# Token halves on TensorE's row tiles, a later second layer, and softmax rows with heads in pairs, in a dynamic convolution with a feed-forward network

## The chip, the cores and the metric

The kernel runs on one core of a Trainium2 chip. The metric is the device time of one execution in microseconds; 881.08 us is the median of three executions before the change (879.11 to 881.46). The profile is of one further execution, whose own time is 880.54 us.

## The reference

A softmax over seven taps per token and head gives the weights of a causal convolution over the last seven tokens; each head weights its own 24 of the 192 channels. The result goes through a feed-forward layer with a squared ReLU.

```python
w = exp(weight_gen - max); w = w / sum(w)                 # (8, 4096, 8 heads, 7 taps)
out[b, s, h, :] = sum_k w[b, s, h, k] * x_pad[b, s + k, h, :]   # 8 heads x 24 channels
h = maximum(out.reshape(32768, 192) @ w_in, 0)            # w_in 192 x 2048
y = (h * h) @ w_out                                       # w_out 2048 x 192, result f32
```

## The kernel before

The 32768 tokens are cut into 64 blocks of 512 (`j`), eight to each of the eight batch entries (`jb` is the place of a block in its entry).

**Softmax.** Per batch entry one table `vd` in DRAM holds, for each token, eight slots per head, of which seven are the normalised weights, skewed so that a row can be read as a band. `exp` runs on ScalarE (L139), the sum and the reciprocal on VectorE (L146, L152), and `scale` (L160) multiplies on GpSimd and writes the result skewed into `v_big`: neighbouring taps land 64 fp16 apart, each value alone. `store` (L172) sends it to DRAM over the queue of SyncE (SP). The first entry is done in four parts of 1024 tokens (`parts`), the first two parts of which stand ahead of the loop and the last two at the start of blocks 0 and 1. Every later entry is done in five chunks during blocks 0 to 4 of the entry before it.

**Convolution.** A block reads its band rows `wr` (SP queue) and its tokens `xt` (GpSimd's queue) three blocks ahead. VectorE multiplies `wr` with a 0/1 mask into a banded matrix `bd` (L223), and TensorE multiplies it with `xt` (L251): 80 small matmuls in four column tiles of 32 columns. Channels 0 to 127 stand in bank 0 of `yp`; channels 128 to 191 stand in bank 1 twice, on partitions 0 to 63 and again on 64 to 127. ScalarE copies both banks to fp16 `y` (L264).

**Feed-forward.** `h` is made in eight pairs of 128 columns (`fp` 0 to 7), each two PSUM banks. The lower matmuls (L274) contract channels 0 to 127 over 512 tokens; the upper ones (L282) contract channels 128 to 191, with the two column groups of a pair side by side in the two 64-row halves of the array. ReLU is on ScalarE (L293), the square on VectorE (L299), the second layer on TensorE (L310), and the result leaves PSUM through VectorE (L320).

**Order.** Every engine runs its instructions in the order in which the code issues them. The eight pairs go in three groups, 0 to 2, 3 to 5, 6 and 7; the second layer of a group is issued behind the first layer of the next group. PSUM has three buffers of two banks, which `h` and `yp` share in turn (`ps_h`), and one for the output `o` (`ps_o`). In the third group the convolution of the next block stands behind both layers' matmuls of that group. In this text lower, upper, conv and second layer are the lines L274, L282, L251 and L310.

## Time and profile before

| | |
|---|---|
| median of three executions | 881.08 us |
| the profiled execution, its own time | 880.54 us |
| its span, first to last instruction | 878.8 us |
| TensorE matmul busy | 796.8 us (91%) |
| VectorE busy | 638.2 us (73%) |
| ScalarE busy | 568.2 us (65%) |
| GpSimd busy | 147.6 us (17%) |
| mean granted TensorE clock | 0.991 of 2.4 GHz |

The span is the time between the first and the last instruction of the core; the execution's own time also has what lies around it. Busy time is the union of the instructions' times, and an instruction's time has its latency in it, so two neighbours on one engine overlap by about 0.1 us (VectorE, ScalarE) or more (TensorE). Idle time is put down to the instruction that ended it.

### The profile page before, as it was taken

The numbers are of one execution on the slowest core, as the hardware profiler recorded it, in microseconds if no ns is written. First come the engines' busy times: TensorE is split into PE (matmuls) and PEld (weight loads), VectorE is DVE, ScalarE is ACT, GpSimd is POOL, SyncE is SP. The second block draws the span as 40 slices with busy tenths as digits, with TensorE's granted clock in tenths as the row PEclk, the third lists the DMA queues.
The fourth block names the chain that finished last, engine by engine and source line by source line (L and its number), as shares of the span: only waits on it lengthen the run. The fifth ranks groups of instructions, "written<-read, shape, count | busy, mean of one in ns | idle before, by whom it ended". The sixth has DMA issues, their size and how long they took to land.

```text
span 878.8 us, 25261 instructions
## 1 busy us (share of the span) xinstructions
PE 796.8 (91%) x11264; PEld 520.6 (59%) x11264; DVE 638.2 (73%) x979; ACT 568.2 (65%) x616; POOL 147.6 (17%) x140
## 2 busy tenths in 40 slices
PE   0678999989998999998999899998999899999997
PEld 0345666655665666665665665665666566666665
DVE  2567787687768787678777778668776878767674
ACT  0346666666676666666666666666667666666764
POOL 5332120123002220112201212012300212000000
PEclk9889999999999999999999999999999999999999
DMA  9522372232713254033622237223271225433111
GB/s 165 116 47 39 60 156 54 37 68 57 141 46 50 52 116 103 25 67 53 144 56 57 35 63 156 48 44 67 51 148 46 45 57 92 78 47 68 41 38 37
DMA packets 123789, 63.03 MB, mean 72 GB/s; under 512 B 87713, under 2 KB 121120, under 8 KB 122912
## 3 DMA queue, kind: packets, MB, share of 16 engines
q0 software_dynamic: 44480, 17.57, 18.0%
q1 hardware_dynamic: 79200, 43.84, 17.4%
q8 instruction: 88, 1.44, 0.7%
q14 instruction: 21, 0.17, 0.1%
HBM read 49.60 MB, written 29.36 MB: 90 GB/s over the span
## 4 chain that ended last, share of the span: by engine, by line
PE 45%; DVE 24%; ACT 14%; issue 13%; DMA 2%; POOL 1%; ACTq 0%; SPq 0%; DVEq 0%; POOLq 0%
PE o L310 23%; PE h L274 12%; DVE g L299 9%; ACT t L293 8%; DVE bd L223 7%; PE h L282 7%; ACT y L264 4%; DVE o_sb L320 4%; PE yp L251 3%; DVE ssum L146 3%; DVE rcp L152 2%; ACT wg L139 2%; DMA wr<-vd 1%; POOL mask L92 0%; DMA vd<-v_small 0%
## 5 line engine op out<-in xcount | busy, mean ns | idle before, releaser
L293 ACT ACTIVATE t<-h 128x1024 f16<-128x1024 f32 x512 | 489.8, 1023 | 282.3 <-PE h L282 264.9
L299 DVE TENSOR_TENSOR g<-t 128x1024 f16<-128x1024 f16 x512 | 383.1, 775 | 102.1 <-ACT t L293 102.1
L310 PE MATMUL o<-w_o,g 128*128 128x192 f16 x4096 | 380.5, 248 | 47.8 <-DVE g L299 41.6
L310 PEld LDWEIGHTS <-g 128*128 128x128 f16 x4096 | 331.8, 98 | 116.4 <-DVE g L299 81.0
L274 PE MATMUL h<-y,w_a 128*128 128x512 f16 x1024 | 259.7, 382 | 8.1 <-ACT t L293 6.9
L223 DVE TENSOR_TENSOR bd<-wr,mask 128x832 f16<-128x832 f16 (+2 forms) x320 | 171.0, 582 | 17.9 <-DMA wr<-vd 17.9
L160 POOL TENSOR_TENSOR v_big<-wg,rcp 128x448 f16<-128x448 f32 (+1 forms) x35 | 81.6, 2330 | 474.2 <-DVE rcp L152 474.2
L274 PEld LDWEIGHTS <-w_a 128*128 128x128 f16 x1024 | 97.9, 98 | 91.0 <-issue 20.0
L282 PE MATMUL h<-y,w_b 64*128 64x512 f16 x1024 | 144.5, 381 | 0.0
L146 DVE TENSOR_REDUCE ssum<-wg 128x64 f32<-128x448 f32 (+2 forms) x39 | 24.7, 633 | 110.0 <-ACT wg L139 110.0
L282 PEld LDWEIGHTS <-w_b 64*128 64x128 f16 x1024 | 34.3, 94 | 97.2 <-issue 82.2
L251 PE MATMUL yp<-bd,xt 128*32 128x104 f16 (+7 forms) x5120 | 71.1, 210 | 21.6 <-DVE bd L223 21.6
L251 PEld LDWEIGHTS <-xt 128*32 128x32 f16 (+3 forms) x5120 | 59.5, 93 | 48.8 <-issue 35.5
L213 POOL DMA_DIRECT2D xt<-in_x_dram x56 | 49.7, 887 | 170.8 <-PE yp L251 170.8
L264 ACT CAST y<-yp 128x1024 f16<-128x1024 f32 x64 | 65.1, 1018 | 19.3 <-PE yp L251 19.3
L320 DVE COPY o_sb<-o 128x768 f32<-128x768 f32 x64 | 60.8, 950 | 3.9 <-PE o L310 1.0
L139 ACT ACTIVATE wg<-wg 128x448 f32<-128x448 f32 (+2 forms) x39 | 23.6, 610 | 2.0 <-DMA wg<-in_weight_gen_dram 2.0
L152 DVE RECIPROCAL rcp<-ssum 128x64 f32<-128x64 f32 (+2 forms) x39 | 22.1, 566 | 1.7
L160 POOL TENSOR_TENSOR v_small<-wg,rcp 128x336 f16<-128x336 f32 (+1 forms) x7 | 13.0, 2025 | 15.9 <-issue 13.9
L211 POOL DMA_DIRECT2D xt<-in_x_dram x8 | 6.0, 751 | 0.0
L205 POOL DMA_DIRECT2D xt<-in_x_dram x8 | 4.8, 606 | 0.0
L92 POOL TENSOR_SCALAR_AFFINE_SELECT mask<-mask 128x104 f16<-128x104 f16 (+2 forms) x6 | 3.1, 509 | 0.4
(14 smaller groups left out, 12.4 us busy)
## 6 DMA issues: line engine op xcount, KB each, us to landing
out_dram<-o_sb SPq DMA_DIRECT2D x64, 384.0 KB, 2.8
xt<-in_x_dram POOLq DMA_DIRECT2D x56, 240.0 KB, 4.0
wg<-in_weight_gen_dram SPq DMA_DIRECT2D x6, 1064.0 KB, 8.2
wr<-vd SPq DMA_DIRECT2D x56, 80.0 KB, 3.0
vd<-v_big SPq DMA_DIRECT2D x7, 512.0 KB, 3.3
wg<-in_weight_gen_dram SPq DMA_DIRECT2D x4, 392.0 KB, 3.7
xt<-in_x_dram POOLq DMA_DIRECT2D x8, 192.0 KB, 6.2
wg<-in_weight_gen_dram SPq DMA_DIRECT2D x1, 896.0 KB, 5.8
```

The source lines that it names most:

```text
L146: nc.vector.tensor_reduce(out=self.ssum[:, i], in_=self.wg[:, i], axis=AxisX, op=AluOp.add)
L160: eng.tensor_tensor(out=bass.AP(tensor=v.tensor, offset=v.offset + i0 * H * SL, ap=[list(v.ap[0]), [H * SL + 1, n], [SL, H], [H * SL, KK]] ...
L213: eng.dma_start(out=dst, in_=rows(src, t0 + BASE, width))
L223: nc.vector.tensor_tensor(out=bd_t[j][:, H * lo : H * hi].rearrange("p (h m c) -> p h m c", h=H, c=SL), in0=wr_t[j][:, i].unsqueeze(2).bro ...
L251: nc.tensor.matmul(out=yp[p0 : p0 + m, ci, lo:hi], lhsT=x_t[j][:, i, 32 * q : 32 * q + m], rhs=bd[:, hb if later else ha, :], start=True, ...
L264: nc.scalar.copy(out=y, in_=yp_t[j])
L274: nc.tensor.matmul(out=h[:, jj, :], lhsT=w_a[:, fc * P : (fc + 1) * P], rhs=y[:, 0, :], start=True, stop=False,)
L282: nc.tensor.matmul(out=h_t[(j, fp)][:, jj, :], lhsT=w_b[r0 : r0 + LO, fc * P : (fc + 1) * P], rhs=y[r0 : r0 + LO, 1, :], start=False, stop ...
L293: nc.scalar.activation(out=t1, in_=h_t[(j, fp)], func=ActF.Relu)
L299: nc.vector.tensor_tensor(out=g, in0=t1, in1=t1, op=AluOp.mult)
L310: nc.tensor.matmul(out=o[:, c // 2, (c % 2) * Dm : (c % 2 + 1) * Dm], lhsT=g_t[(j, fp)][:, jj, c * P : (c + 1) * P], rhs=w_o[:, fc, :], st ...
L320: nc.vector.tensor_copy(out=o_sb, in_=o_t[j][:, :, 0 : 2 * Dm])
```

## The change

**Token halves.** `h` and its successors are laid out by halves of 256 tokens: `[half][column group][256]`. The lower matmuls have 256 columns instead of 512 and are twice as many. The upper channels of the first 256 tokens stand on partitions 0 to 63 of `yp`'s second bank and those of the last 256 tokens on 64 to 127, so that nothing is held twice; the two row halves of the array work on the two token halves with the same weights. The convolution has 64 matmuls instead of 80, and ScalarE copies 768 columns of `yp` instead of 1024.

**Heads in pairs.** The slots of `vd`, `wr` and `bd` hold two heads side by side. `exp` writes into a tile of its own in that order, `scale` is four instructions per chunk (one per pair of heads) whose output has two fp16 next to each other, and the convolution reads every second element of the band. The mask is twice as wide.

**Order.** The second layer of pairs 0 to 2 stands behind the first layer of the second group as before, that of 3 and 4 behind the third group, and that of 5 to 7 behind the first group of the next block. The convolution stands between the lower and the upper matmuls of the third group, and its PSUM buffer is taken ahead of theirs. In the steady loop `exp` stands behind the first group's ReLUs, and sum, reciprocal and `scale`, the last now on VectorE, behind the second group's squares. An entry is spread over seven blocks (8, 8, 8, 4, 4, 4 and 2 rows; the first over five). Ahead of the loop the loads, masks and parts are issued in another order. `g` has 6 buffers instead of 8, `bd` 3 instead of 2.

```diff
+            if lo == 0:
+                self.ex = p_wg.tile([P, self.rh, HP, KK, 2], f32, name=f"ex{self.r}")
+                self.ssum = p_sm.tile([P, self.rh, HP, 2], f32, name=f"ssum{self.r}")
+                self.rcp = p_sm.tile([P, self.rh, HP, 2], f32, name=f"rcp{self.r}")
+            nc.scalar.activation(
+                out=self.ex[:, lo:hi].rearrange("p r g k e -> p (r g) k e"),
+                in_=self.wg[:, lo:hi].rearrange("p r (g e) k -> p (r g) k e", e=2),
+                func=ActF.Exp,
...
+        def scale(self, lo, hi, eng):
+
+            v = self.v
+            while lo < hi:
+                n = min(SL - lo % SL, hi - lo)
+                for g in range(HP):
+                    eng.tensor_tensor(
+                        out=bass.AP(
+                            tensor=v.tensor,
+                            offset=v.offset + lo * H * SL + lo % SL * 2 + g * SL * 2,
+                            ap=[list(v.ap[0]), [H * SL + 2, n], [H * SL, KK], [1, 2]],
+                        ),
+                        in0=self.ex[:, lo : lo + n, g],
+                        in1=self.rcp[:, lo : lo + n, g].unsqueeze(2).broadcast_to((P, n, KK, 2)),
+                        op=AluOp.mult,
+                    )
+                lo += n
...
+        shape = (P, HP, n // SL, 2 * SL)
...
+            out=bd_t[j][:, H * lo : H * hi].rearrange("p (g m c) -> p g m c", g=HP, c=2 * SL),
+            in0=wr_t[j][:, i].unsqueeze(2).broadcast_to(shape),
+            in1=m.rearrange("p (m c) e -> p m (c e)", c=SL).unsqueeze(1).broadcast_to(shape),
...
+    def conv_pieces():
...
+                for q in range(4):
+                    yield later, i, q, 32 * q, 0, lo, lo, hi
+                for half in (0, 1):
+                    a, b = max(lo, TH * half), min(hi, TH * (half + 1))
+                    if a < b:
+                        for q in (4, 5):
+                            yield later, i, q, 32 * (q - 4) + LO * half, 1, a - TH * half, a, b
...
+    def st_conv(j):
+        yp = yp_t[j]
+        for later, i, q, p0, ci, col, a, b in conv_pieces():
...
+            bd = bd_t[j][:, H * lo : H * hi].rearrange("p (g c e) -> p g e c", g=HP, e=2)
...
+                rhs=bd[:, h // 2, h % 2, a - lo : b - lo],
...
+        y = p_y.tile([P, TB + TH], f16, name="y")
...
+        nc.scalar.copy(out=y, in_=yp_t[j].rearrange("p a c -> p (a c)")[:, 0 : TB + TH])
...
+    def st_mm1_lower(j, fps):
         y = y_t[j]
         for fp in fps:
...
+                for half in range(2):
+                    nc.tensor.matmul(
+                        out=h[:, half, jj, :],
+                        lhsT=w_a[:, fc * P : (fc + 1) * P],
+                        rhs=y[:, half * TH : (half + 1) * TH],
+                        start=(jj == 0), stop=False, skip_group_check=True,
...
+    def st_mm1_upper(j, fps):
+        y = y_t[j]
         for fp in fps:
...
+                for half, r0 in enumerate((0, LO)):
+                    nc.tensor.matmul(
+                        out=h_t[(j, fp)][:, half, jj, :],
+                        lhsT=w_b[r0 : r0 + LO, fc * P : (fc + 1) * P],
+                        rhs=y[r0 : r0 + LO, TB : TB + TH],
+                        start=False, stop=(jj == 1), skip_group_check=True,
+                        tile_position=(r0, 0),
...
+                        lhsT=g_t[(j, fp)][:, half, jj, cc * P : (cc + 1) * P],
...
+    def softmax_whole(s, engines):
+        s.exp(0, s.rh)
+        s.recip(0, s.rh)
+        for n, lo in enumerate(range(0, s.rh, SL)):
+            s.scale(lo, min(lo + SL, s.rh), engines[n % len(engines)])
+        s.store(nc.sync)
+
+
+
+    G0, G1, G2 = (0, 1, 2), (3, 4, 5), (6, 7)
+    LATE = (5, 6, 7)
+    UNIT = 4
...
-        for s in parts[:2]:
-            s.load(nc.sync)
+        parts[0].load(nc.sync)
+        nc.vector.memset(v_small[0], 0.0)
+        band_mask(mask0, 0)
+        softmax_whole(parts[0], (nc.vector, nc.gpsimd))
+        st_load(0)
         load_w_in()
-        band_mask(mask0, 0)
...
+        parts[1].load(nc.sync)
         st_load(1)
...
-        whole_part(parts[1], (nc.gpsimd,))
+        band_mask(mask[:, 0 : bounds[1]], -starts[0])
+        softmax_whole(parts[1], (nc.gpsimd,))
+        for s in parts[2:]:
+            s.load(nc.sync)
         st_load(2)
...
+            nxt = Softmax(1, 0, R, v_big, new_vd(1))
             nxt.load(nc.sync)
...
-                whole_part(parts[2 + j], (nc.gpsimd,))
...
+                softmax_whole(parts[2 + j], (nc.gpsimd,))
             if nxt and jb == 5:
                 nxt.store(nc.sync)
-            if nxt and jb == 6:
-                nxt = after if b + 2 < B else None
+                nxt, done = None, 0
+                if b + 2 < B:
+                    nxt = Softmax(b + 2, 0, R, v_big, new_vd(b + 2))
+                    nxt.load(nc.sync)
+            lo = hi = 0
+            if nxt and jb != 5:
+                left = (4 - jb) % NBB + 1
+                lo = done
+                hi = done = min(lo + -(-(nxt.rh - lo) // (UNIT * left)) * UNIT, nxt.rh)
...
+            st_mm1_lower(j, G0)
+            st_mm1_upper(j, G0)
+            if j:
+                st_mm2(j - 1, LATE)
+            for fp in G0:
+                st_relu(j, fp)
+            if lo < hi:
+                nxt.exp(lo, hi)
+            if more:
+                for i in (0, 1, 2):
+                    st_band(j + 1, i)
+            st_sq(j, 0)
+            st_sq(j, 1)
+            if j:
+                st_o_evac(j - 1)
+            st_sq(j, 2)
+            if more:
+                for i in (3, 4):
+                    st_band(j + 1, i)
+
+            st_mm1_lower(j, G1)
+            st_mm1_upper(j, G1)
+            st_mm2(j, (0, 1, 2))
+            for fp in G1:
+                st_relu(j, fp)
+                st_sq(j, fp)
+            if lo < hi:
+                nxt.recip(lo, hi)
+                nxt.scale(lo, hi, nc.vector)
+
+            if more:
+                st_conv_alloc(j + 1)
+            st_mm1_lower(j, G2)
+            if more:
+                st_conv(j + 1)
+                st_y_evac(j + 1)
+            st_mm1_upper(j, G2)
+            st_mm2(j, (3, 4))
+            for fp in G2:
+                st_relu(j, fp)
+                st_sq(j, fp)
+        st_mm2(NBLK - 1, LATE)
```

On VectorE, from the end of one block's second group to the start of the next block (`ssum` and `rcp` are the softmax's sum and reciprocal, `g` a square, `bd` the band), it stood before:

```order
L299 TENSOR_TENSOR g<-t_826 128x1024
L299 TENSOR_TENSOR g<-t_828 128x1024
L299 TENSOR_TENSOR g<-t_830 128x1024
L146 TENSOR_REDUCE ssum_478<-wg_257 128x64
L152 RECIPROCAL rcp_479<-ssum_478 128x64
L299 TENSOR_TENSOR g<-t_955 128x1024
L299 TENSOR_TENSOR g<-t_957 128x1024
L223 TENSOR_TENSOR bd<-wr,mask 128x832 x2
L223 TENSOR_TENSOR bd<-wr,mask 128x768
```

and stands now:

```order
L339 TENSOR_TENSOR g<-t_908 128x1024
L339 TENSOR_TENSOR g<-t_912 128x1024
L150 TENSOR_REDUCE ssum_310<-ex_309 128x64
L155 RECIPROCAL rcp_311<-ssum_310 128x64
L163 TENSOR_TENSOR v_big<-ex_309,rcp_311 128x8x7x2 x4
L339 TENSOR_TENSOR g<-t_1023 128x1024
L339 TENSOR_TENSOR g<-t_1027 128x1024
L229 TENSOR_TENSOR bd<-wr,mask 128x832 x2
L229 TENSOR_TENSOR bd<-wr,mask 128x768
L339 TENSOR_TENSOR g<-t_1086 128x1024
L339 TENSOR_TENSOR g<-t_1088 128x1024
```

Sum, reciprocal and the new `scale` stand ahead of the last two squares as sum and reciprocal did, but `exp`, on which they wait, moved. On ScalarE, over the third group and the softmax behind it (`t` is a ReLU's output, `y` the copy of the convolution), it stood before:

```order
L293 ACTIVATE t_955<-h 128x1024
L293 ACTIVATE t_957<-h 128x1024
L264 CAST y<-yp 128x1024
L139 ACTIVATE wg_257<-wg_257 128x448
L293 ACTIVATE t_1004<-h 128x1024
L293 ACTIVATE t_1006<-h 128x1024
```

and stands now, from the first group's three ReLUs on:

```order
L333 ACTIVATE t_830<-h 128x1024
L333 ACTIVATE t_832<-h 128x1024
L333 ACTIVATE t_834<-h 128x1024
L142 ACTIVATE ex_309<-wg_255 128x448
L333 ACTIVATE t_904<-h 128x1024
L333 ACTIVATE t_908<-h 128x1024
L333 ACTIVATE t_912<-h 128x1024
L279 CAST y<-yp 128x768
L333 ACTIVATE t_1023<-h 128x1024
L333 ACTIVATE t_1027<-h 128x1024
```

`exp` moved from behind the copy of `y` to behind the first group's ReLUs, and the copy stands ahead of the third group's ReLUs instead of behind them. On SP's queue at the start (`wg8` are loads for the four parts of the first entry, `wg32` that of the second entry, `vd` a store, `wr` the band rows of a block), it stood before:

```order
L124 DMA wg8_104<-in_weight_gen_dram 128x784
L124 DMA wg8_106<-in_weight_gen_dram 128x784
L172 DMA vd_103<-v_small0_99 128x512
L205 DMA wr_140<-vd_103 128x64
L211 DMA wr_140<-vd_103 128x4x64
L124 DMA wg8_145<-in_weight_gen_dram 128x784
L124 DMA wg8_147<-in_weight_gen_dram 128x784
L213 DMA wr_150<-vd_103 128x5x64
L172 DMA vd_103<-v_small1_100 128x512
L213 DMA wr_252<-vd_103 128x5x64
L124 DMA wg32_257<-in_weight_gen_dram 128x2128
```

and stands now:

```order
L126 DMA wg8_104<-in_weight_gen_dram 128x784
L177 DMA vd_103<-v_small0_99 128x512
L210 DMA wr_126<-vd_103 128x64
L216 DMA wr_126<-vd_103 128x4x64
L126 DMA wg8_146<-in_weight_gen_dram 128x784
L218 DMA wr_149<-vd_103 128x5x64
L177 DMA vd_103<-v_small1_100 128x512
L126 DMA wg8_245<-in_weight_gen_dram 128x784
L126 DMA wg8_247<-in_weight_gen_dram 128x784
L218 DMA wr_250<-vd_103 128x5x64
L126 DMA wg32_255<-in_weight_gen_dram 128x2128
```

The band rows of block 1 moved ahead of the loads for parts 2 and 3, and those two loads moved behind the store of part 1. On ScalarE at the start stands now (numbers tell the parts apart; `ex8_257` is part 2):

```order
L142 ACTIVATE ex8_110<-wg8_104 128x784
L279 CAST y_224<-yp_159 128x768
L142 ACTIVATE ex8_230<-wg8_146 128x784
L142 ACTIVATE ex8_257<-wg8_245 128x784
L333 ACTIVATE t1_303<-h_276 128x1024
L333 ACTIVATE t1_305<-h_281 128x1024
L333 ACTIVATE t1_307<-h_286 128x1024
L142 ACTIVATE ex32_309<-wg32_255 128x448
L333 ACTIVATE t1_377<-h_325 128x1024
```

Part 2's `exp` stands ahead of block 0's first ReLU, as it did before, and the second entry's first `exp` moved to between block 0's first and second group.

## Rows read from the trace of the kernel before

**Rows 1.** Busy time by stage: blocks 0 and 1, two loop blocks, last block.
```profile
25.29:48.05 22.76, 15.66 (x161) 8.87 (x161) 10.91 (x16) 10.38 (x12) 8.39 (x6) 0.85 0.51 111
48.05:68.30 20.25, 14.78 (x178) 9.74 (x177) 14.92 (x18) 9.98 (x12) 6.82 (x4) 0.83 0.28 47
408.94:422.50 13.56, 12.35 (x179) 8.08 (x178) 10.76 (x16) 9.04 (x11) 2.92 (x2) 1.00 0.26 48
435.24:447.74 12.50, 12.27 (x179) 8.05 (x177) 8.69 (x16) 8.55 (x9) 0.85 (x1) 1.00 0.44 97
861.28:878.84 17.56, 12.74 (x114) 8.36 (x112) 7.27 (x10) 7.65 (x8) 0.00 (x0) 0.94 0.13 46
```

**Rows 2.** Timeline (start us, us, instruction, xcount): TensorE in a block without softmax.
```profile
435.24 1.46 PE L274 MATMUL h<-y,w_a 128*128 128x512 f16 x6
436.63 0.82 PE L282 MATMUL h<-y,w_b 64*128 64x512 f16 x6
...
438.71 1.03 PE L274 MATMUL h<-y,w_a 128*128 128x512 f16 x4
439.96 0.59 PE L274 MATMUL h<-y,w_a 128*128 128x512 f16 x2 [0.23 <-ACT t L293]
440.49 0.82 PE L282 MATMUL h<-y,w_b 64*128 64x512 f16 x6
441.24 2.15 PE L310 MATMUL o<-w_o,g 128*128 128x192 f16 x24
443.23 1.03 PE L274 MATMUL h<-y,w_a 128*128 128x512 f16 x4
444.19 0.61 PE L282 MATMUL h<-y,w_b 64*128 64x512 f16 x4
444.73 1.09 PE L251 MATMUL yp<-bd,xt 128*32 128x104 f16 x80
445.75 2.15 PE L310 MATMUL o<-w_o,g 128*128 128x192 f16 x24
```

**Rows 3.** The same view, ScalarE in the second group of that block.
```profile
440.92 2.85 ACT L293 ACTIVATE t<-h 128x1024 f16<-128x1024 f32 x3 [1.01 <-PE h L282]
```

**Rows 4.** The same view, all engines, a block that starts with softmax work.
```profile
409.18 0.62 DVE L146 TENSOR_REDUCE ssum<-wg 128x64 f32<-128x448 f32 x1 [2.76 <-ACT wg L139]
...
410.30 2.72 DVE L299 TENSOR_TENSOR g<-t 128x1024 f16<-128x1024 f16 x2
...
410.57 2.43 POOL L160 TENSOR_TENSOR v_big<-wg,rcp 128x448 f16<-128x448 f32 x1 [10.64 <-DVE rcp L152]
...
413.07 0.83 PE L310 MATMUL o<-w_o,g 128*128 128x192 f16 x8 [1.16 <-DVE g L299]
```

**Rows 5.** Groups by line and shape (count, busy us, mean ns, idle before).
```profile
L264 ACT CAST y<-yp 128x1024 f16<-128x1024 f32 x64 | 65.1, 1018 | 19.3 <-PE yp L251 19.3
...
L160 DVE TENSOR_TENSOR v_small<-wg,rcp 128x448 f16<-128x448 f32 x1 | 2.2, 2153 | 0.0
```

**Rows 6.** Timeline, all engines, from the start to block 0.
```profile
9.41 1.69 POOL L160 TENSOR_TENSOR v_small<-wg,rcp 128x336 f16<-128x336 f32 x1
...
14.33 17.77 SPq L124 DMA_DIRECT2D wg<-in_weight_gen_dram  x2
...
28.03 3.71 POOL L160 TENSOR_TENSOR v_small<-wg,rcp 128x448 f16<-128x448 f32 x2 [13.93 <-issue]
...
28.59 2.85 ACT L293 ACTIVATE t<-h 128x1024 f16<-128x1024 f32 x3 [1.85 <-PE h L282]
...
39.32 4.02 PE L310 MATMUL o<-w_o,g 128*128 128x192 f16 x24 [6.48 <-DVE g L299]
```

**Rows 7.** Timeline, all engines, block 1.
```profile
53.88 3.98 DVE L223 TENSOR_TENSOR bd<-wr,mask 128x832 f16<-128x832 f16 x3
```

**Rows 8.** DMA issues by line: count, KB each, median us to landing.
```profile
wg<-in_weight_gen_dram SPq DMA_DIRECT2D x6, 1064.0 KB, 8.2
...
wg<-in_weight_gen_dram SPq DMA_DIRECT2D x4, 392.0 KB, 3.7
```

193 lines of the change are left out of this document (55 added, 138 removed).

## The prediction

> **What bounds the kernel now.** I read first the busy time by stage, then TensorE's timeline, then what the late instructions waited for. From block 2 (at 68.30 us) to block 63 (at 861.28 us) the loop has only three lengths [rows 1]: a block without softmax takes 12.50 us, one that starts behind softmax work about 13.56, and the one behind an entry's last, smaller chunk 12.74. With 27 of the second kind and 7 of the third, 61 x 12.50 + 27 x 1.06 + 7 x 0.24 = 792.8 us, which is the 792.98 between the two starts. Ahead of that stand 25.29 us until the first lower matmul and blocks 0 and 1 with 22.76 and 20.25 us; behind it stands the last block's 17.56.
>
> TensorE bounds the 12.50 us. Its rows follow each other without a gap but one [rows 2]: lower plus its switch takes 1.39 us in the first group (435.24 to 436.63) and 1.78 in the second (438.71 to 440.49), because the last pair waits for a PSUM buffer that ScalarE's ReLU has yet to empty. That is 0.39 us; the other 12.11 are the stream itself. At 1.00 granted clock (the 2.4 GHz level) 192 columns take 1.99 / 24 = 0.083 us (441.24 to 443.23) [rows 2], 3 ns above 192 / 2.4 GHz.
>
> The extra 1.06 us is a chain through VectorE [rows 4]. Sum and reciprocal stand ahead of the last two squares and the sum waits 2.76 us for `exp`; the two squares then take 2.72 us, while GpSimd's `scale` runs for 2.43 beside them, and the second layer of pair 7 starts 1.16 us late. In block 1 three band products take 3.98 us beside GpSimd's `scale` [rows 7].
>
> **The loop, part by part.**
>
> *Stream of TensorE.* Same columns in the lower, upper and second layer. 16 more lower starts and 8 more upper pairs, at the 3 ns above, cost 24 x 0.003 = 0.07 us. The convolution still goes in four passes per piece of the band, since pairs of column tiles stand idle where half a bank's channels were; only the middle piece saves 2 x 48 columns, 0.04 us. Switches between full array, row tiles and column tiles stay seven per block. 12.11 + 0.07 - 0.04 = 12.14.
>
> *The step of two.* In every TensorE row of the trace the moving operand is contiguous, so no row prices a read at every second fp16. The convolution streams for about 0.92 us (444.73 to 445.75, less the switch) [rows 2]. Bounds: nothing, as in these rows, and double, +0.92 us per block; a gain beyond the saved columns is excluded, since the columns are no fewer. I take nothing, the value of the nearest row. The Trainium skill's page "SBUF — State Buffer" (Door 1: The DMA port swizzle, the note on cachelines) says that SBUF is read in lines of 16 bytes, that two hits per line keep full bandwidth, and that 2-byte elements may be strided freely up to eight. A step of two has four hits, so by that rule the convolution keeps 0.92 us; no row here shows it. The same rule speaks of `scale`: single values 128 bytes apart have one hit per line, which agrees with the 2.15 us for 448 values in the row below, and two side by side would have two.
>
> *The stall of 0.39* goes: 24 second-layer matmuls instead of 16 stand between the first group's upper and the second group's lower, 0.66 us more for the ReLUs. Two others come. (a) `yp` now takes the buffer that pair 6 had, so pair 7 waits for pair 5's ReLU. From the second group's first upper matmul (440.49) the three ReLUs end after 3.28 us (440.92 + 2.85) [rows 3]; TensorE is through upper and second layer after 2.74 (443.23) and through pair 6 after 3.18 [rows 2]. With the handover: 0.15 us. (b) The copy of `y` stands ahead of pairs 6 and 7's ReLUs. From conv's start TensorE needs 1.02 conv, 0.54 upper (444.19 to 444.73), 1.32 for 16 second-layer matmuls and 0.87 for two pairs of the next lower, 3.75 in sum. ScalarE: conv's end at 1.09, the copy, two ReLUs of 0.92. The copy takes 1.02 us for 1024 columns [rows 5]; for 768 it lies between 0.76 (in proportion) and 1.02; I take 0.85, which gives 3.87 with latencies and 0.12 us of waiting. 12.14 + 0.15 + 0.12 = 12.41, so 12.40.
>
> *Softmax on VectorE.* `exp` stands where ScalarE idles over 1 us ahead of the second group's ReLUs [rows 3], and a sum issued a third of a block later does not wait. `scale` leaves GpSimd, and with it what the two squares lost beside it [rows 4]. It adds four starts on VectorE. 448 values took 2.15 us in one instruction [rows 5] (GpSimd's masks ran beside it); bounds for four are 0.7 (the sum's rate, 448 values in 0.62 us [rows 4], and the starts) and 2.5 (the old price and three more starts); I take 1.3, half the old price and the starts. VectorE is busy 8.69 us in a block without softmax [rows 1]; with sum and reciprocal (409.18 to 410.30, 1.12 [rows 4]) and 1.3 it has 11.1 of 12.4, and its work lies between pair 5's square and pair 6's ReLU, which now comes only after conv and copy. So all blocks take 12.40 us, and that holds up to about 2.5 us of `scale`. Bands keep shape and type, and I price them as before.
>
> The loop: 61 x 12.40 = 756.4 us, 36.6 less; 30 of these are the softmax's.
>
> **The start.** Before, GpSimd's half of part 0 stood behind all masks (9.41) and ended at 11.10, right ahead of the store [rows 6]. Now VectorE's and GpSimd's halves start together behind the reciprocal, at about 6.8 (VectorE's row of 2.15 us ended ahead of 9.41), and end near 8.7: -2.4 us for all up to the first lower, 22.9. Then comes a worse order. Part 1: copy, `exp`, sum, reciprocal as before from 25.1 to 28.0, now 22.5 to 25.4; GpSimd's eight calls, of which no row shows one, between half and twice the 3.71 us of the two old ones [rows 6]; I take 3.7, to 29.1. Only then can SP store part 1 and load parts 2 and 3 behind it; 392 KB land 3.7 us later [rows 8], about 33.3. Part 2's `exp` (0.86) stands ahead of the first ReLU, which starts at 34.2 instead of 28.59 [rows 6]. The load of 1064 KB, fourth behind, takes 8.2 us [rows 8] and lands near 40.6; its `exp` stands ahead of pair 3's ReLU. Three ReLUs, conv, upper and two pairs of second layer (0.6 + 2.8 + 1.0 + 0.6 + 1.3, and 1.1 between) put block 1 at 48.0. Before it was 48.05: SP was stuck 17.77 us on the load of part 3 with block 1's band rows behind it, and TensorE waited 6.48 for the squares [rows 6]. So that wait is replaced by another. In block 1 part 3's `exp`, sum and GpSimd's `scale` still collide with the bands [rows 7]; taken off are the chunk's chain, 1.06 as in the loop, and by my estimate 2.9 of the waits, as block 1's bands no longer stand behind two softmax chains in a row; bounds are none of it and all 7.75 over 12.50. That makes 16.3 instead of 20.25. The granted clock of 0.85 and 0.83 in these blocks [rows 1] stays too: behind the long wait 24 second-layer matmuls took 4.02 us instead of 2.15 [rows 2, 6], the 1.2 GHz level. Block 2 starts at 64.3.
>
> **Sum.** 64.3 + 756.4 + 17.56 [rows 1] = 838.3 us of span. The profiled execution had 880.54 around a span of 878.8, 1.74 more; the median was 0.54 above it: 840.6, say 840 us.
>
> **The rivals.**
> B, *the step of two halves the convolution's rate.* For it: TensorE is the bound, and nothing hides 0.92 us there. Against it: no row. 62 x 0.92 = 57 us more: 897 us. From 1.7 times the old stream (41 us over 62 blocks) the kernel is slower than before.
> C, *VectorE becomes the bound.* If `scale` takes 3.0 us, 0.5 over the 2.5 that fit, pairs 0 to 2's squares come late in each of the 47 blocks that carry a chunk: 47 x 0.5 = 23 us, 863. Its old price in one piece speaks for a high cost, the 3.8 us that VectorE idles in a block without softmax [rows 1] against.
> D, *the start loses.* GpSimd's calls at twice 3.71 us hold SP, ScalarE and VectorE through block 1: +3.7 for the loads and as much again beside the bands, 848.
> E, *the halves do not pair.* If the two row tiles' matmuls on half the columns ran one behind the other, upper would take twice its 1.7 us per block: 62 x 1.7 = 105 us more. Against it: the same two tiles run six matmuls in 0.75 us with their switch (440.49 to 441.24) [rows 2], each pair in two banks of PSUM, which stays so.
>
> **How the numbers follow.** Forecast 64 in 100, with its own range of 824 to 858 (0.15 us per block either way is 9 us; the start, 7). B 17, of which 13 end above 884 and 4 between; C 9; D 9; E 1. A difference under 0.3% cannot be told from none here. Slower by more than that: B's 13, E and 1 of C: 15 in 100. Within: 3, where B or C stops halfway. Faster: 82. The range of 822 to 884 leaves out B's and E's 14 and some 5 below or between.
>
> **What would show it.** Right: blocks of 12.3 to 12.5 us alike with and without softmax; no wait of the second layer for a square; waits of about 0.1 us for ReLU at the last lower of the first and third group; conv's row at about 1.1 us; block 1 near 48, with ScalarE idle until a DMA ahead of block 0's first ReLU. Wrong: a conv row near 2 us (B), second layer of pair 0 waiting for a square or for the copy of `o` (C), block 2 beyond 70 us (D).

## The result and the profile after

The changed kernel takes 821.3 us (median of four executions, 821.07 to 822.54) against 880.81 for the kernel before in the same session: a ratio of 0.933, with a 95% interval of 0.9314 to 0.9346. The profiled execution has a span of 819.6 us instead of 878.8. The forecast was 840 us, with a range of 822 to 884: its direction was right, its gain a third too small, and the time lies just below the range.

The busy time by stage (stretch in us, its length, then PE, PEld, DVE, ACT and POOL busy with their instruction counts, granted clock, DMA share, GB/s) for block 0, block 1, one loop block and the last block, to be laid beside [rows 1]:

```profile
24.25:47.16 22.91, 14.23 (x169) 10.09 (x169) 14.09 (x22) 9.58 (x12) 12.02 (x21) 0.78 0.86 164
47.16:60.88 13.72, 12.20 (x194) 10.38 (x193) 12.96 (x24) 9.66 (x12) 6.91 (x11) 1.00 0.42 72
449.48:461.62 12.14, 12.14 (x195) 10.30 (x194) 9.94 (x21) 8.65 (x11) 0.86 (x1) 1.00 0.36 62
801.67:819.60 17.93, 13.35 (x155) 11.36 (x152) 8.65 (x12) 8.52 (x9) 0.00 (x0) 1.00 0.13 45
```

Each of the 61 loop blocks now takes 12.13 to 12.16 us, whether it carries softmax or not; before they took 13.00 in the mean. TensorE is busy for all of the third stretch. The chain of waits says the same: TensorE had 45% of it before, and now

```profile
PE 94%; DVE 1%; DMA 1%; ACT 1%; POOL 0%; issue 0%; SPq 0%; ACTq 0%; DVEq 0%
```

TensorE's timeline of that loop block (start, us, instruction, xcount), against [rows 2]:

```profile
449.48 1.53 PE L291 MATMUL h<-y,w_a 128*128 128x256 f16 x12
450.94 0.83 PE L304 MATMUL h<-y,w_b 64*128 64x256 f16 x12
451.70 2.15 PE L322 MATMUL o<-w_o,g 128*128 128x192 f16 x24
453.69 1.48 PE L291 MATMUL h<-y,w_a 128*128 128x256 f16 x12
...
457.85 1.04 PE L291 MATMUL h<-y,w_a 128*128 128x256 f16 x8
458.81 1.00 PE L266 MATMUL yp<-bd,xt 128*32 128x104 f16 x64
459.74 0.61 PE L304 MATMUL h<-y,w_b 64*128 64x256 f16 x8
460.29 1.49 PE L322 MATMUL o<-w_o,g 128*128 128x192 f16 x16
461.62 0.60 PE L291 MATMUL h<-y,w_a 128*128 128x256 f16 x4
```

The second group's lower (453.69) runs without the 0.39 us gap. The third group's lower takes 0.96 us to the convolution's start, as before, so nothing waits there. The first group's row is 0.05 us longer than the second's: that is all that these rows leave of waiting. The convolution streams for 0.93 us (458.81 to 459.74) instead of 1.02.

The groups behind single terms (count, busy us, mean ns, idle before), against [rows 5]; the `scale` of the loop mixes chunks of several sizes here:

```profile
L279 ACT CAST y<-yp 128x768 f16<-128x768 f32 x64 | 51.1, 798 | 113.7 <-PE yp L266 113.7
...
L163 DVE TENSOR_TENSOR v_big<-ex,rcp 128x112 f16<-128x112 f32 (+3 forms) x188 | 32.7, 236 | 1.6
...
L90 POOL TENSOR_SCALAR_AFFINE_SELECT mask<-mask 128x208 f16<-128x208 f16 (+2 forms) x6 | 6.9, 1146 | 0.4
```

The start, all engines, against [rows 6]:

```profile
22.11 0.63 DVE L229 TENSOR_TENSOR bd<-wr,mask 128x896 f16<-128x896 f16 x1 [1.00 <-POOL mask L94]
...
27.07 2.61 POOL L163 TENSOR_TENSOR v_small<-ex,rcp 128x112 f16<-128x112 f32 x8 [0.46 <-DVE rcp L155]
...
30.12 0.92 SPq L126 DMA_DIRECT2D wg<-in_weight_gen_dram  x2
...
35.06 0.93 ACT L142 ACTIVATE ex<-wg 128x784 f32<-128x784 f32 x1 [10.03 <-DMA wg<-in_weight_gen_dram]
35.90 2.83 ACT L333 ACTIVATE t<-h 128x1024 f16<-128x1024 f32 x3
...
36.96 2.84 PE L291 MATMUL h<-y,w_a 128*128 128x256 f16 x12 [8.68 <-ACT t L333]
...
39.95 0.62 ACT L142 ACTIVATE ex<-wg 128x448 f32<-128x448 f32 x1 [1.22 <-DMA wg<-in_weight_gen_dram]
```

The bands wait for GpSimd's masks, which cost 1.1 us per call now that they are twice as wide in pairs. SP issues parts 2 and 3 only at 30.12; ScalarE then stands still for 10.03 us with three ReLUs queued behind part 2's `exp`, and TensorE for 8.68.

### The profile page after: what moved, and what is told of

It is laid out like the page before. It is cut to its first block, busy times and chain, and to the rows that moved or that the text cites. A ratio compares the mean times of both kernels' runs of the same rounds, so it can differ in the third digit from the quotient of the medians.

```text
span 819.6 us, 27464 instructions
## 1 busy us (share of the span) xinstructions
PE 783.1 (96%) x12288; PEld 662.1 (81%) x12288; DVE 642.0 (78%) x1194; ACT 557.1 (68%) x628; POOL 90.4 (11%) x126
## 4 chain that ended last, share of the span: by engine, by line
PE 94%; DVE 1%; DMA 1%; ACT 1%; POOL 0%; issue 0%; SPq 0%; ACTq 0%; DVEq 0%
PE o L322 43%; PE h L291 27%; PE h L304 16%; PE yp L266 7%; DMA wg<-in_weight_gen_dram 1%; ACT t L333 0%; DVE o_sb L343 0%; DVE bd L229 0%; ACT ex L142 0%; DVE g L339 0%; POOL v_small L163 0%; DVE ssum L150 0%; DVE rcp L155 0%; SPq L177 0%; ACTq L142 0%
## 5 line engine op out<-in xcount | busy, mean ns | idle before, releaser
L339 DVE TENSOR_TENSOR g<-t 128x1024 f16<-128x1024 f16 x512 | 353.9, 692 | 144.2 <-ACT t L333 139.3
L291 PE MATMUL h<-y,w_a 128*128 128x256 f16 x2048 | 260.9, 274 | 9.6 <-ACT t L333 8.7
L291 PEld LDWEIGHTS <-w_a 128*128 128x128 f16 x2048 | 197.7, 98 | 34.1 <-issue 10.4
L304 PE MATMUL h<-y,w_b 64*128 64x256 f16 x2048 | 146.4, 273 | 0.0
L279 ACT CAST y<-yp 128x768 f16<-128x768 f32 x64 | 51.1, 798 | 113.7 <-PE yp L266 113.7
L304 PEld LDWEIGHTS <-w_b 64*128 64x128 f16 x2048 | 84.7, 95 | 41.9 <-issue 27.6
L266 PE MATMUL yp<-bd,xt 128*32 128x104 f16 (+14 forms) x4096 | 65.9, 209 | 20.8 <-DVE bd L229 20.7
L150 DVE TENSOR_REDUCE ssum<-ex 128x64 f32<-128x448 f32 (+4 forms) x51 | 26.3, 515 | 13.4 <-ACT ex L142 13.3
L142 ACT ACTIVATE ex<-wg 128x448 f32<-128x448 f32 (+4 forms) x51 | 27.5, 540 | 13.1 <-DMA wg<-in_weight_gen_dram 13.1
L163 DVE TENSOR_TENSOR v_big<-ex,rcp 128x112 f16<-128x112 f32 (+3 forms) x188 | 32.7, 236 | 1.6
```

The source lines that it names most:

```text
L142: nc.scalar.activation(out=self.ex[:, lo:hi].rearrange("p r g k e -> p (r g) k e"), in_=self.wg[:, lo:hi].rearrange("p r (g e) k -> p (r g ...
L163: eng.tensor_tensor(out=bass.AP(tensor=v.tensor, offset=v.offset + lo * H * SL + lo % SL * 2 + g * SL * 2, ap=[list(v.ap[0]), [H * SL + 2, ...
L266: nc.tensor.matmul(out=yp[p0 : p0 + m, ci, col : col + b - a], lhsT=x_t[j][:, i, 32 * q : 32 * q + m], rhs=bd[:, h // 2, h % 2, a - lo : b ...
L279: nc.scalar.copy(out=y, in_=yp_t[j].rearrange("p a c -> p (a c)")[:, 0 : TB + TH])
L291: nc.tensor.matmul(out=h[:, half, jj, :], lhsT=w_a[:, fc * P : (fc + 1) * P], rhs=y[:, half * TH : (half + 1) * TH], start=(jj == 0), stop ...
L304: nc.tensor.matmul(out=h_t[(j, fp)][:, half, jj, :], lhsT=w_b[r0 : r0 + LO, fc * P : (fc + 1) * P], rhs=y[r0 : r0 + LO, TB : TB + TH], sta ...
```

## The experiments

**The stall (a): which buffer the convolution takes.** In the built program a PSUM buffer is handed out at its tile's first write, in the order of release. So the line that takes `yp`'s buffer early has no effect: `yp` gets pair 5's buffer and pair 7 pair 4's, long free. This run gives `yp` a first write at the early place:

```diff
+                if fp == 3 and more:
+                    st_conv_alloc(j + 1)
+                    nc.vector.memset(yp_t[j + 1][:, 1, TB - 1 : TB], 0.0)
...
-            if more:
-                st_conv_alloc(j + 1)
```

> The changed kernel, with the convolution's PSUM buffer claimed by a one-column VectorE memset right behind pair 3's ReLU, so that yp takes pair 3's buffer and pair 7 gets pair 5's; nothing else moves, and the written column is used by nobody. By the forecast's stall (a) this is what the changed kernel was thought to do already: lower of pair 7 then waits for pair 5's ReLU, 0.1 to 0.15 us per block, 62 blocks, 6 to 9 us: 827 to 830 us against 821.3. By the rival (the stall would not have come even with that buffer, because ReLUs and TensorE were priced wrongly) the third group's lower keeps its 0.97 us and the time stays within 1 us of 821.3, as the memset lies in VectorE's idle time.

Measured: 831.48 us, every loop block 12.29 instead of 12.145. The third group's lower in its timeline takes 1.11 us to the convolution's start instead of 0.96:

```profile
451.97 1.19 PE L291 MATMUL h<-y,w_a 128*128 128x256 f16 x8
...
453.08 1.00 PE L266 MATMUL yp<-bd,xt 128*32 128x104 f16 x64
```

So the forecast's 0.15 us is what that wait costs (0.14); the wait was put into a kernel that does not have it.

**The stall (b): the width of the copy.**

The copy takes columns 0 to 511 of `yp`, and 256 to 767 once more:

```diff
-        y = p_y.tile([P, TB + TH], f16, name="y")
-        y_t[j] = y
-        nc.scalar.copy(out=y, in_=yp_t[j].rearrange("p a c -> p (a c)")[:, 0 : TB + TH])
+        y = p_y.tile([P, 2, TB], f16, name="y")
+        y_t[j] = y.rearrange("p a c -> p (a c)")
+        yp = yp_t[j]
+        nc.scalar.copy(
+            out=y,
+            in_=bass.AP(
+                tensor=yp.tensor, offset=yp.offset, ap=[list(yp.ap[0]), [TH, 2], [1, TB]]
+            ),
+        )
...
-                        rhs=y[r0 : r0 + LO, TB : TB + TH],
+                        rhs=y[r0 : r0 + LO, TB + TH : 2 * TB],
```

> The changed kernel with the copy of y widened from 768 to 1024 columns (256 of them copied twice, from the same PSUM buffer); all else is kept. Theory: the copy stands ahead of pair 6's and 7's ReLUs, and the third pair of the next block's first group waits for pair 7's ReLU; the copy then takes 1.02 us instead of 0.80 and the wait grows from 0.05 by 0.22 to 0.27 us, as in the kernel before with the new order (1.68 us of lower instead of 1.39): blocks of 12.36 us, 61 x 0.22 = 13 us more, 832 to 837 us. So the forecast's term (b) had the right mechanism and a copy of 0.85 instead of 0.80, and the order's 12.40 against 12.145 is this copy. Rival: the new order's 12.40 us came from the old row tiles, then the time stays within 3 us of 821.3.

Measured: 835.34 us, 12.36 us per block. The first group's lower takes 1.74 us where the changed kernel takes 1.53 and the second group 1.47:

```profile
435.94 1.47 PE L297 MATMUL h<-y,w_a 128*128 128x256 f16 x12
...
443.86 1.74 PE L297 MATMUL h<-y,w_a 128*128 128x256 f16 x12
```

The mechanism is as forecast. With 0.80 us the copy ends nearly in time; the wide copy takes 1.01 us, and TensorE pays all of the 0.21 us between them (0.215 per block).

**The order, alone and in parts.** Four runs. First the changed kernel with the old split of the second layer (`LATE = (6, 7)`, pairs 3 to 5 behind the third group):

> The changed kernel with the second layer split as in the kernel before: pairs 3 to 5 behind the third group, 6 and 7 behind the next block's first group. If the 16 to 24 second-layer matmuls between the first group's upper and the second group's lower are what removed the stall of 0.39 us, it comes back: 0.66 us less cover there, about +0.35 us per block less the 0.05 that the third tile of the first group waits now, x 61 = 18 to 24 us: 839 to 845 us. Rival: the stall went because the ReLUs lie otherwise (the copy of y and exp were moved on ScalarE), then the second group's lower stays at 1.41 us and the time within 3 us of 821.3.

Measured: 841.02 us, 12.46 per block; the gap is back in the second group's lower, which takes 1.78 us to the next row (452.84), as in [rows 2]:

```profile
451.06 1.04 PE L291 MATMUL h<-y,w_a 128*128 128x256 f16 x8
452.31 0.60 PE L291 MATMUL h<-y,w_a 128*128 128x256 f16 x4 [0.21 <-ACT t L333]
```

Then the same split alone, put into the kernel before:

```diff
-                if before:
-                    st_mm2(*before)
+                if gi == 0 and j:
+                    st_mm2(j - 1, (5, 6, 7))
+                elif gi:
+                    st_mm2(j, ((0, 1, 2), (3, 4))[gi - 1])
...
-                before = (j, fps)
-        st_mm2(*before)
+        st_mm2(NBLK - 1, (5, 6, 7))
```

> The kernel before with one thing of the change alone: second layer of pairs 0 to 2, 3 and 4, then 5 to 7 behind the next block's first group. Theory: the stall of 0.39 us at the second group's lower goes in all blocks (62 x 0.39 = 24 us) and another may come at the next block's first group, since the copy of y still stands behind the ReLUs; the softmax's 1.06 us in 27 blocks is not touched in its cause, but the two late squares (pairs 6 and 7) are now needed 0.66 us later, which would take 0.5 to 0.66 us off each of these. Together 24 to 40 us less: 841 to 857 us. Rival: the cover only moves the wait to another group, then the time stays within 5 us of 881.

Measured: 882.34 us, a ratio of 1.0019 (1.0007 to 1.0031): no gain, the rival. TensorE's timeline shows where it went:

```profile
349.47 1.46 PE L274 MATMUL h<-y,w_a 128*128 128x512 f16 x6
...
356.12 1.49 PE L310 MATMUL o<-w_o,g 128*128 128x192 f16 x16
357.89 0.38 PE L274 MATMUL h<-y,w_a 128*128 128x512 f16 x1 [0.28 <-ACT y L264]
```

The gap at the second group is gone (1.46). But the 8 matmuls that moved had covered the copy of `y`, which stands behind two ReLUs, and the next block's lower waits for it. Blocks take 12.55 instead of 12.50, and 13.56 with softmax as before: there too the second layer still waits 0.73 us for a square and the lower 0.28 for the copy. In the new order, where convolution and copy stand ahead of the upper matmuls and the ReLUs, the same split is worth 0.32 us per block, by the run before this one.

Third, the kernel before with the softmax's new place alone (`exp` behind the first group's ReLUs, the rest behind the second group's squares):

> The kernel before with one thing of the change alone: exp behind the first group's ReLUs, sum, reciprocal and scale (GpSimd still, single values) behind the second group's squares. Theory: the sum no longer waits 2.76 us for exp, so of the 1.06 us in 27 blocks and 0.24 in 7, 30 us in sum, most goes: 852 to 862 us. Rival: GpSimd's scale beside the squares is the cost (2.72 us for two squares instead of 1.7), then it slows other squares instead and at least half of the 30 us stays: 866 to 881 us.

Measured: 849.25 us, a ratio of 0.964 (0.9625 to 0.9656); all loop blocks take 12.50 us. This is the largest part of the gain. A block with a chunk, in the view by stage:

```profile
392.23:404.73 12.50, 12.27 (x178) 8.05 (x177) 10.97 (x17) 8.92 (x10) 3.36 (x5) 1.00 0.28 52
```

Its TensorE is busy for as long as in the block without softmax in [rows 1], so GpSimd's `scale` did not slow TensorE from there.

Fourth, the kernel before with the whole order of the loop, old tiles, single values, `scale` on GpSimd and the old start (`conv_and_copy` is called between lower and upper; the lines that move the softmax are left out):

```diff
-                st_mm1(j, fps)
-                if gi == NG - 1 and j + 1 < NBLK:
-                    st_conv(j + 1)
-                if before:
-                    st_mm2(*before)
+                last = gi == NG - 1 and j + 1 < NBLK
+                st_mm1(j, fps, conv_and_copy if last else None)
+                if gi:
+                    st_mm2(j, ((0, 1, 2), (3, 4))[gi - 1])
+                elif j:
+                    st_mm2(j - 1, (5, 6, 7))
```

> The kernel before with the loop's whole order from the change (later second layer, convolution between lower and upper of the third group with the copy of y ahead of the ReLUs, exp and softmax at their new places), but the old tiles, the old bands, single values and scale on GpSimd, and the old start. Theory O (order alone brings the loop's gain): the two stalls and the softmax's share go, but the copy of y has 1024 columns and takes 1.02 us instead of 0.80, so the third pair of the next block's first group waits about 0.2 us longer than the 0.05 seen; stream 12.11, in sum 12.1 to 12.4 us in every block, and with the old start (61 to 68 us to block 2) 822 to 845 us. Theory P (the pairs and token halves are needed, because scale on GpSimd with single values or the wider copy costs more at the new places): blocks of 12.5 us or more, at least 849 us, as with the softmax's place alone.

Measured: 845.34 us, 12.40 us in every loop block. Its first lower waits 0.29 us for pair 7's ReLU behind the copy of 1024 columns (1.75 against 1.46 us in the second group):

```profile
328.51 1.75 PE L274 MATMUL h<-y,w_a 128*128 128x512 f16 x6
...
332.93 1.46 PE L274 MATMUL h<-y,w_a 128*128 128x512 f16 x6
```

The 12.40 us are the upper end of theory O's range, and the time lies 0.3 us above it; neither 12.1 nor P's 12.5 is right. Between 12.40 and the changed kernel's 12.145 lies the token halves' part, and the run with the wide copy puts 0.215 of these 0.255 us down to the 256 columns that the copy no longer has.

**The softmax put back late** in the changed kernel:

```diff
-            if lo < hi:
-                nxt.exp(lo, hi)
...
-            if lo < hi:
-                nxt.recip(lo, hi)
-                nxt.scale(lo, hi, nc.vector)
...
             for fp in G2:
                 st_relu(j, fp)
+            if lo < hi:
+                nxt.exp(lo, hi)
+                nxt.recip(lo, hi)
+                nxt.scale(lo, hi, nc.vector)
+            for fp in G2:
                 st_sq(j, fp)
```

> The changed kernel with exp, sum, reciprocal and scale put back to where the kernel before had them, behind the third group's ReLUs and ahead of the squares of pairs 6 and 7; scale stays on VectorE with heads in pairs. Theory: sum waits for exp, and the two squares stand behind 0.47 to 0.94 us of scale and 1.1 us of sum and reciprocal; the second layer of pairs 5 to 7 is needed about 0.66 us later than before, so the stall is 0.5 to 1.5 us in each of about 47 blocks with a chunk: 845 to 890 us. Rival: with the later second layer and the fast scale the place no longer matters: within 4 us of 821.3.

Measured: 888.98 us, 0.9% above the kernel before (ratio 1.0092, 1.0076 to 1.0108). A block with 8 rows takes 14.04 us, one with 4 rows 13.16:

```profile
254.36 0.63 ACT L142 ACTIVATE ex<-wg 128x448 f32<-128x448 f32 x1
255.02 0.62 DVE L150 TENSOR_REDUCE ssum<-ex 128x64 f32<-128x448 f32 x1 [3.82 <-ACT ex L142]
...
257.01 1.29 DVE L339 TENSOR_TENSOR g<-t 128x1024 f16<-128x1024 f16 x2
257.75 1.49 PE L322 MATMUL o<-w_o,g 128*128 128x192 f16 x16 [1.09 <-DVE g L339]
...
261.89 2.14 PE L322 MATMUL o<-w_o,g 128*128 128x192 f16 x24 [0.57 <-DVE o_sb L343]
```

The delay is paid twice: pairs 6 and 7 wait for their squares, and the copy of `o`, behind these on VectorE and ahead of the next second layer, comes late as well. A block loses 1.90 us here and 1.06 in [rows 4]; by the rows the 0.75 us of `scale` (from 256.26, behind the reciprocal, to the squares at 257.01) that VectorE now does ahead of the squares is most of the difference. That was not tried apart.

**Who scales, and pairs against single values.** `scale` of the loop on GpSimd (`nxt.scale(lo, hi, nc.gpsimd)`):

> The changed kernel with the loop's scale (four instructions per chunk, heads in pairs) on GpSimd instead of VectorE, at the same place. Theory: TensorE bounds the loop with slack on VectorE (78% busy), so moving the scale off it gains nothing; GpSimd beside VectorE slows the squares of pairs 6 and 7 and the bands, as in block 1 before (3.98 us for three band products). The squares have 1 to 2 us of slack, so the time is 821 to 830 us. Rival: the shared port costs more than the slack, each of 47 blocks loses 0.5 us or more: over 845 us.

Measured: 821.27 us, blocks of 12.15. The slowing that the theory expected is not there: the mean of a square is 0.697 us instead of 0.692, and that of a band stays at 0.583. And `scale` on VectorE with single values:

```diff
-                            offset=v.offset + lo * H * SL + lo % SL * 2 + g * SL * 2,
-                            ap=[list(v.ap[0]), [H * SL + 2, n], [H * SL, KK], [1, 2]],
+                            offset=v.offset + lo * H * SL + lo % SL + g * SL * 2,
+                            ap=[list(v.ap[0]), [H * SL + 1, n], [H * SL, KK], [SL, 2]],
```

> The changed kernel with scale still on VectorE, but writing single values (two heads 16 bytes apart, as in the old layout) instead of two side by side; the convolution then reads some weights of other tokens, so that part of the result differs. Theory: the single value is what made 448 values take 2.15 us; four instructions then take about 2.2 us per chunk of 8 rows instead of 0.94, still within the 2.5 us that VectorE has spare in a block, so the loop's 8-row blocks stay at 12.15 or gain up to 0.3 us: 821 to 830 us. Rival: it was GpSimd's masks beside it that made the 2.15 us, then single values cost as little as pairs, about 0.24 us per instruction, and the time is 821.3.

Measured: 823.83 us; in the timeline the four instructions of 8 rows take 2.15 us instead of 0.83 (first the changed kernel, then this one),

```profile
46.41 0.83 DVE L163 TENSOR_TENSOR v_big<-ex,rcp 128x112 f16<-128x112 f32 x4
```

```profile
134.07 2.15 DVE L163 TENSOR_TENSOR v_big<-ex,rcp 128x112 f16<-128x112 f32 x4
```

and the loop's blocks stay at 12.15. Of 1.8 us more span, 1.7 are ahead of block 2, which starts at 62.55; that is no sign of a cost, since block 2 starts anywhere from 60.71 to 62.69 us in the profiles of kernels with the same start. So single values do cost 2.6 times as much, and in this loop neither that nor the engine matters.

**The step of the convolution.** Two lines each: the band read side by side, at step four, at step eight. The edit for step four:

```diff
-            bd = bd_t[j][:, H * lo : H * hi].rearrange("p (g c e) -> p g e c", g=HP, e=2)
+            bd = bd_t[j][:, H * lo : H * hi].rearrange("p (g c e) -> p g e c", g=2, e=4)
...
-                rhs=bd[:, h // 2, h % 2, a - lo : b - lo],
+                rhs=bd[:, h // 4, h % 4, a - lo : b - lo],
```

> The changed kernel with the convolution reading the same number of band values side by side instead of at every second fp16; the values read are others, so this part of the result differs. Forecast: a step of two costs nothing, the convolution's row stays at 0.93 us and the time at 821.3 within 1 us. Rival B in part: the step costs some rate, then the convolution's row falls below 0.93 us (by half if the rate were halved) and the time falls by 62 times that.

> The changed kernel with the convolution reading its band at step four (8 bytes) instead of two; the values read are others, so this part of the result differs. Side by side the convolution took 0.97 us by its rows, at step two 1.01, at step eight 3.32. By the Trainium skill, page SBUF - State Buffer (note on cachelines under Door 1), a line of 16 bytes is still hit twice, so full bandwidth: 0.97 to 1.1 us, 821 to 826 us. Rival from the rows alone: if the rate falls with the bytes used per line, step four would lie between, at 1.6 to 1.8 us: 858 to 871 us.

> The changed kernel with the convolution reading its band values eight fp16 apart (16 bytes) instead of two; the values read are others, so this part of the result differs. By the Trainium skill, page SBUF - State Buffer (note on cachelines under Door 1), each line of 16 bytes is then hit once, and full bandwidth wants two hits; the page leaves the size of the loss open, and a halved rate would show as a convolution of about 1.8 us. By numbers of the traces alone: a halved rate is +0.9 us x 62 = +56 us (877 us); if TensorE reads so few rows per cycle that the step does not matter, the convolution stays at 0.93 us and the time at 821.3 within 1 us. I expect something between for the first and lean to no change.

Measured: 820.45, 869.66 and 967.62 us; the loop's blocks take 12.11, 12.90 and 14.45. The convolution and the row behind it, side by side, then at step four, then at step eight:

```profile
459.61 0.97 PE L266 MATMUL yp<-bd,xt 128*32 128x104 f16 x64
460.51 0.61 PE L304 MATMUL h<-y,w_b 64*128 64x256 f16 x8
```

```profile
446.07 1.76 PE L266 MATMUL yp<-bd,xt 128*32 128x104 f16 x64
447.77 0.61 PE L304 MATMUL h<-y,w_b 64*128 64x256 f16 x8
```

```profile
452.55 3.31 PE L266 MATMUL yp<-bd,xt 128*32 128x104 f16 x64
455.78 0.61 PE L304 MATMUL h<-y,w_b 64*128 64x256 f16 x8
```

By the starts: 0.90 us at step one, 0.93 at two, 1.70 at four, 3.23 at eight. So the step of two costs next to nothing, as forecast; step four came out at its rival, and at step eight the lean to no change was wrong. The second layer, which streams alone, with its weights read at step four (and eight) tells whether the four column tiles share a limit. The edit for step four:

```diff
-                        rhs=w_o[:, fc, :],
+                        rhs=w_o.rearrange("p c (m e) -> p (c m) e", e=4)[
+                            :, fc : fc + Dm, 0
+                        ],
```

> The changed kernel with the second layer's 192 streamed weights read at step four (8 bytes) instead of side by side; the values read are others, so the second layer's result differs. The convolution lost at step four (1.76 us instead of 1.01), but there four column tiles read at a time, each its own band. Theory S (one stream has a limit of its own, by bytes used of what is read): 24 matmuls take about 3.4 us instead of 1.99, 64 matmuls per block 3.8 us more, 62 x 3.8 = +236 us, about 1057 us. Theory F (the four streams share what one stream alone could have): the second layer keeps 1.99 us per 24 and the time is 821 to 825 us.

> As the run before, at step eight (16 bytes); again the second layer's result differs. Theory S: 24 matmuls take about 6.5 us (the convolution's 3.32 against 1.01), +740 us in sum. Theory F: four streams at step four lost about 1.8 times and at step eight 3.3 times, so one stream alone at step eight takes no more than one of the four at step two: 1.99 us per 24 and 821 to 825 us. The Trainium skill, page SBUF - State Buffer (note on cachelines under Door 1), has one hit per line here and so less than full bandwidth, without a figure.

Measured: 1183.71 and 2151.33 us: theory S. Of each kernel one row of the second layer and the next one:

```profile
588.26 4.32 PE L322 MATMUL o<-w_o,g 128*128 128x192 f16 x24
592.40 1.49 PE L291 MATMUL h<-y,w_a 128*128 128x256 f16 x12
```

```profile
1020.27 8.32 PE L322 MATMUL o<-w_o,g 128*128 128x192 f16 x24
1028.42 2.42 PE L291 MATMUL h<-y,w_a 128*128 128x256 f16 x12
```

24 matmuls take 4.14 and 8.15 us instead of 1.99: 2.1 and 4.1 times. Theory S was right in kind and too small in size (3.4 and 6.5 us). At step eight TensorE's granted clock also falls, and the rows that read side by side take longer by it (2.42 us for 12 lower matmuls instead of 1.49). The second layer's own time does not follow the clock, as two of its stretches of 24 show, the first at 0.70 and the second at 0.85:

```profile
1020.27:1028.42 8.15, 8.15 (x27) 2.95 (x26) 1.39 (x2) 2.70 (x4) 0.00 (x0) 0.70 0.01 2
1031.53:1039.67 8.14, 8.14 (x26) 2.85 (x25) 3.99 (x9) 2.53 (x3) 0.00 (x0) 0.85 0.10 21
```

So a single stream has the limit by itself, and of the steps tried (one, two, four, eight) two is the last that is nearly free.

**The start.** The loads of part 2 and of the second entry's table moved ahead of part 1's store; then, on top, the masks built at single width and widened on VectorE; then, on top, in blocks 0 and 1 alone, the first three bands behind the first group's squares.

```diff
         st_load(1)
+        parts[2].load(nc.sync)
+        nxt = Softmax(1, 0, R, v_big, new_vd(1))
+        nxt.load(nc.sync)
...
-        for s in parts[2:]:
-            s.load(nc.sync)
+        parts[3].load(nc.sync)
...
-        nxt, done = None, 0
-        if B > 1:
-            nxt = Softmax(1, 0, R, v_big, new_vd(1))
-            nxt.load(nc.sync)
+        done = 0
```

```diff
-        nc.gpsimd.memset(t, 1.0)
+        m = one[:, at : at + n]
+        nc.gpsimd.memset(m, 1.0)
...
+        nc.vector.tensor_copy(out=t, in_=m.unsqueeze(2).broadcast_to((P, n, 2)))
```

```diff
-            if more:
+            if j > 1 and more:
                 for i in (0, 1, 2):
...
-                for i in (3, 4):
+                for i in range(0 if j < 2 else 3, NT):
```

> The changed kernel with the loads of part 2 and of the second entry's table issued ahead of part 1's store on SP's queue instead of behind it. Theory: block 0's wait of 8.7 us for its first ReLUs is ScalarE held by part 2's exp, whose load was issued late; with the load early it falls to 2 us or less, and block 2 starts 6 to 9 us earlier: 812 to 816 us. Rival: ScalarE is then held by the next thing late (GpSimd's eight calls, or the exp of part 3), and less than 3 us is won: over 818 us.

> The run with the early loads, and the band masks built single-width on GpSimd and widened by a VectorE copy instead of built double-width on GpSimd. Theory: the first bands waited for GpSimd's masks (1.04 us per call instead of 0.27), so the first lower starts 1 to 2 us earlier than in the run with the early loads: 810 to 815 us. Rival: the wait is for the band rows' DMA anyway, then it is the same time within 1 us.

> The fastest version so far (early loads, single-width masks) with the band products of blocks 1 and 2 issued behind the first group's squares instead of ahead of them, in blocks 0 and 1 only. Theory: in block 0 three bands beside GpSimd's scale take 4.07 us ahead of the squares and TensorE waits 2.94 us, and what follows runs at a lower clock; in block 1 it waits 1.53 us for the copy of o, which stands behind bands and squares. Both shrink or go: 3 to 6 us less, 808 to 811 us. Rival: the bands then make the convolution late and the wait moves there, within 1.5 us of 814.1.

Measured: 815.78, 814.07 and 809.08 us (ratios to the kernel before of 0.9257, 0.9242 and 0.9184, the last with 0.9169 to 0.92). With the early loads the first ReLUs start at 26.92 instead of 35.90 and block 0 takes 17.79 us. The forecast of 812 to 816 held, though block 2 starts 5.75 us earlier and not 6 to 9; part of the 8.68 us turned into a new wait, as three bands beside GpSimd's `scale` take 4.07 us ahead of the squares:

```profile
29.39 4.07 DVE L229 TENSOR_TENSOR bd<-wr,mask 128x832 f16<-128x832 f16 x3
...
34.12 3.68 PE L322 MATMUL o<-w_o,g 128*128 128x192 f16 x24 [2.94 <-DVE g L339]
```

The single-width masks bring the first lower from 23.62 to 21.81; the profiles with wide masks have it at 23.37 to 24.39. In the times the two versions' intervals overlap (0.9242 to 0.9272 and 0.9222 to 0.9261). Moving the bands takes the last wait away; blocks 0 and 1 of that version:

```profile
22.03:35.66 13.63, 12.96 (x168) 9.40 (x168) 12.50 (x17) 9.58 (x12) 9.60 (x18) 1.00 1.01 171
35.67:48.51 12.84, 12.30 (x194) 10.43 (x193) 12.67 (x23) 9.67 (x12) 7.36 (x11) 1.00 0.39 51
```

This version beats both kernels.

## Why the forecast missed

The span fell by 59.2 us. By the runs (a step of the loop block counts 61 times in the span):

| part | loop block, us | span, us |
|---|---|---|
| kernel before, mean | 13.00 | |
| softmax moved | 12.50 | -30.5 |
| rest of the order | 12.40 | -6.1 |
| token halves: copy of 768 columns | 12.185 | -13.1 |
| token halves and step of two: the rest | 12.145 | -2.4 |
| up to block 2 (68.30 to 60.88) | | -7.4 |
| last block (17.56 to 17.93) | | +0.4 |

The forecast's span of 838.3 us was 18.7 us too long: 15.6 of these lie in the loop and 3.4 ahead of block 2, and the last block took 0.4 more than forecast.

*The step that failed* is the loop's stall (a), "`yp` now takes the buffer that pair 6 had, so pair 7 waits for pair 5's ReLU". It takes pair 5's, and the wait is not there: the forecast's 0.15 us x 61 = 9 us. The order of the calls was read as the order in which buffers are given; the program gives them at first use.

*Mis-sized terms.* (b) had the right mechanism; the copy took 0.80 us, not 0.85, and the wait is 0.05 us, not 0.12: 4 us. The convolution lost 0.09 us and not 0.04, which is 3 us; no run shows why it lost more than the columns of the middle piece. Together with (a) that is, rounded, the loop's 15.6 us (61 x 0.255).

*Softmax:* right. The 30 us of [rows 4] are its place (30.5 by the run with that alone), and blocks are alike. Four `scale` instructions took 0.83 us against an estimate of 1.3, inside its bounds of 0.7 to 2.5. The limit of 2.5 us was not tested: the 2.15 of single values still fit.

*The step of two:* right, at 0.03 us per block against nothing. The Trainium skill's page "SBUF — State Buffer" (Door 1, the note on cachelines) would have let 2-byte elements be strided up to eight; for TensorE's moving operand the runs do not agree. Steps of four and eight cost 2.1 and 4.1 times in a stream that runs alone. The forecast's value came from contiguous rows and was right at the edge: rival B was one doubling of the step away.

*The start:* first lower 24.25 against 22.9, because the masks in pairs cost GpSimd 1.1 us per call and the price of their width was left out. Block 1 at 47.16 against 48.0: the wait was where the forecast put it (8.68 us, ScalarE held 10.03 us by a load). Its terms were off both ways: eight GpSimd calls 2.61 us and not 3.7, part 2's load in use at 35.06 and not at about 33.3, the second entry's at 39.95 and not 40.6. That block 1 still started within 0.9 us of the forecast is in part luck. Block 1 took 13.72 against 16.3: three bands took 1.88 us, not 3.98 as in [rows 7], and the granted clock was back at 1.00 (the 2.4 GHz level), where the forecast left it at 0.83. In block 0 it is 0.78, behind the 8.68 us wait; in the version without that wait 1.00. The price of bands beside GpSimd is open: in block 1 here they took 1.88 us (1.55 in a loop block) and GpSimd's eight calls beside them 4.33, while in block 0 with the early loads the bands took 4.07 and the calls 2.61, their time in part 1. No run shows what decides which of the two loses.

*Rivals:* C did not come, nor would it have at 2.15 us of `scale`. D's price was the calls at 7.4 us; ahead of the loads they took 2.61, and beside VectorE's work in blocks 0 and 1 5.48 and 4.33. E did not come: the upper matmuls take 0.76 us for three pairs, as before.

## What to carry to other kernels

Before a wait for a pooled buffer is priced, look up in the built program which tile hands it over. Cover that is moved to one gap is taken from another: the later second layer alone was worth nothing (1.0019), in the new order 0.32 us per block; so follow what the moved work used to hide. On the engine ahead of the bottleneck, work that stands in front of what the bottleneck waits for is paid in full (the copy's 256 columns), while work that fits into the engine's slack is free (`scale` behind the second group, 0.83 or 2.15 us, on either engine).
